# Order of TensorE's steps in an attention pair: the second score group directly behind the first, the third ahead of the mixing

## The chip, the cores and the metric

One core of one Trainium2 chip. The metric is the device time of one execution in microseconds; for the kernel before it is the median of three runs.

## What is computed

Causal attention over 2 batches, 12 heads, 448 tokens and head size 64, then a token-and-channel-mixing block, then a block with a Fourier transform over tokens and channels, a normalisation and a two-layer perceptron, all in fp32:

```python
scores = scale * np.matmul(q, k.transpose(0, 1, 3, 2))
scores = np.where(mask, -1000000000.0, scores)
attn = softmax(scores)                      # rows: exp(s - max) / (sum + 1e-9)
x = np.matmul(attn, v)                      # to (batch, token, channel)
h = np.maximum(x.transpose(0, 2, 1) @ w_tok1, 0.0) @ w_tok2
u = x + h.transpose(0, 2, 1)
x = u + np.maximum(u @ w_ch1, 0.0) @ w_ch2
u = x + real(fft(fft(x, tokens), channels))
out = u + np.maximum(norm(u) @ w2_ch1, 0.0) @ w2_ch2
```

(The softmax, norm and fft lines are abbreviated.)

## The kernel before

Values are split into a high and a low part in a rounded fp32 type, and a product is three passes: high x high, high x low, low x high. The channel weights of the blocks come as 64-bit words and are converted on the chip: `convert_steps` (L77) is one ScalarE instruction (L83), then VectorE's L85 and L86, L90, L94, then a ScalarE copy (L100) and a GpSimd subtraction (L101).

**Attention stage.** The 24 (batch, head) problems are done as 12 pairs. A pair n goes through these steps:

- `prep(n)` (L221): loads q and k by two DMAs on SP's queue and splits them: ScalarE L229 and L231, GpSimd L230, VectorE L235.
- `scores(n, g)` (L243) for the three score groups g = 0, 1, 2. The 448 query rows are four blocks of 112; by causality block i needs only the first 112 (i + 1) keys. Group 0 is blocks 0 and 1, group 1 is block 2, group 2 is block 3. Each group does its matmuls (L261) for both heads, adds the mask by small matmuls (L274), then VectorE reduces for the negative maximum (L278) and ScalarE takes the exponentials with their sums (L287, one instruction and one read of the accumulator per block and head: four in group 0, two in the others).
- `transposes(n, u)` (L292), u = 0 to 4: five groups of four 112x112 transposes of the exponentials on TensorE (L300), each copied out of its bank, for u = 1, 3 by ScalarE (L305), for u = 0, 2, 4 by VectorE (L307), into the one buffer `pt`.
- `pv(n)` (L309): P times V in 16 matmuls (L315), of which the second half reads transposed groups 2 to 4; ScalarE copies the result out (L320).
- `finish(n)` (L322): four transposes back (L336), division by the row sums on VectorE (L332, L333, L338), a split by VectorE L344 and GpSimd L345.

The steps of different pairs are interleaved in the loop at L465. In iteration n the scores are those of pair n, the transposes those of pair n - 1, P times V and `finish` those of pair n - 2. `next_mix()` (L407) takes one step of the token-mixing block off a list that is filled after every third pair: `mix_first` and `mix_second` in iterations 5, 8 and 11 (matmuls L361, evacuated by ScalarE L367 and VectorE L368, and transposes L373 copied by ScalarE L376), and three `mix_out` (L395, added by VectorE L397) in the two iterations after. `weights(after)` (L455) issues one third of the conversion of one weight tile, behind the instructions named, each on its own engine: `mark[2]` is the last score reduction traced (VectorE) and `mark[3]` the last exponential (ScalarE); the number of such steps in an iteration is in `parts` (L461).

**What sets the order.** TensorE's instructions run in the order in which the loop calls them (L464). The order of the other engines is chosen by the framework's planner from priorities, estimated durations and dependencies, and is fixed when the program is built. PSUM has eight banks. Score groups take turns at two pairs of banks (`spair`, L143; in pair 0 group 2 takes two single ones); everything else in this stage takes turns at the other four (`ybank`, L140). Whoever takes a bank waits until what was in it has been read.

The order of TensorE in one iteration before (for 2 <= n < 12): score group 0 of n; P times V of n - 2; score group 1 of n; transposed groups 0 and 1 of n - 1; a mixing step, if any; transposed group 2; score group 2 of n; transposed groups 3 and 4; a mixing step; the transposes of `finish(n - 2)`.

Of the kernel before, what the change touches and what calls it, by code (L numbers as in the profile page):

```python
# [43 lines left out]
def fused_kernel(ctx: ExitStack, tc: tile.TileContext, qk, v, w1, w2, wa, wb, wc, wd, fa, fa0, fb, out):  # L44
# [7 lines left out]
    def small(pool, tag, **kw):  # L52
        t = pool.tile([TS, 16], F32, tag=tag, name=tag, **kw)
        return t[:, : 2 * NI].rearrange("p (i e o) -> p i e o", e=2, o=1)
# [17 lines left out]
    def fetch(src):  # L72
        w = stage_pool[0].tile(list(src.shape), I64, tag="w", name="w", bufs=2)
        nc.sync.dma_start(out=w, in_=src)
        return w
# [64 lines left out]
    def ybank():  # L140
        return psum[:, take("y", 4)]

    def spair():  # L143
        k = 4 + 2 * take("s", 2)
        return psum[:, k : k + 2]
# [41 lines left out]
    with ExitStack() as actx:  # L187
# [33 lines left out]
        def prep(n):  # L221
            c = Pair()
            pairs[n] = c
            b, hp = n // 6, n % 6
            c.kh, c.kl, c.qh, c.ql = [kq.tile([128, S], F32R, tag=t, name=t) for t in ("kh", "kl", "qh", "ql")]
            k32, q32 = stage(n), stage(n)
            nc.sync.dma_start(out=k32, in_=qk[b, hp, :, 1])
            nc.sync.dma_start(out=q32, in_=qk[b, hp, :, 0])
            act.copy(c.kh, k32)  # L229
            (pool if n else vec).tensor_tensor(out=c.kl, in0=k32, in1=f(c.kh), op=ALU.subtract)  # L230
            act.activation(out=c.qh, in_=q32, func=AF.Copy, scale=0.125)  # L231
            with ExitStack() as order:
                if n == 1:
                    order.enter_context(tc.issue_after(mark[2]))
                vec.scalar_tensor_tensor(  # L235
                    out=c.ql, in0=q32, scalar=0.125, in1=f(c.qh), op0=ALU.mult, op1=ALU.subtract
                )
# [5 lines left out]
        def scores(n, g):  # L243
            c = pairs[n]
            if g == 0:
                c.ssum = small(tiny, "ssum")
                c.nmx = small(ap, "nmx")
                c.p = ap.tile([TS, 2, 1120], F32, tag="p", name="p")
            if n or g < 2:
                sp = spair()  # L250
                se = [sp[:TS, e] for e in range(2)]
            else:
                se = [ybank()[:TS] for e in range(2)]
            cols = ((256, 0), (0,), (0,))[g]
            blocks = ((0, 1), (2,), (3,))[g]
            for i, c0 in zip(blocks, cols):
                w = max(256, TS * (i + 1))
                for m, (qt, kt) in enumerate(((c.qh, c.kh), (c.qh, c.kl), (c.ql, c.kh))):
                    for e in range(2):
                        he = slice(D * e, D * e + D)  # L260
                        mm(  # L261
                            se[e][:, c0 : c0 + w], lhsT=qt[he, i * TS : (i + 1) * TS], rhs=kt[he, :w],
                            start=m == 0 and i != 1, stop=False, skip_group_check=True,
                        )
            for hb in range(2):
                for e in range(2):
                    he = slice(D * e, D * e + TS // 2)
                    if g == 0:
                        dst = se[e][:, TS : TS + 288].rearrange("p (i n) -> p i n", i=2)[:, :, :TS]
                        rhs = maskb[he, hb]  # L270
                    else:
                        dst = se[e][:, blocks[0] * TS : (blocks[0] + 1) * TS]
                        rhs = maskb[he, hb, 0]
                    mm(dst, lhsT=identb[he, hb], rhs=rhs, start=False, stop=hb == 1, skip_group_check=True)  # L274
            for i, c0 in zip(blocks, cols):
                w = TS * (i + 1)
                if n or g < 2:
                    mark[2] = vec.tensor_reduce(  # L278
                        out=c.nmx[:, i], in_=sp[:TS, :, c0 : c0 + w], axis=AX.X, op=ALU.max, negate=True
                    ).ins  # L280
                else:
                    for e in range(2):
                        vec.tensor_reduce(out=c.nmx[:, i, e], in_=se[e][:, :w], axis=AX.X, op=ALU.max, negate=True)
            for i, c0 in zip(blocks, cols):
                w = TS * (i + 1)
                for e in range(2):
                    mark[3] = act.activation(  # L287
                        out=c.p[:, e, OFF[i] : OFF[i] + w], in_=se[e][:, c0 : c0 + w], func=AF.Exp,
                        bias=c.nmx[:, i, e], scale=1.0, accum_out=c.ssum[:, i, e],
                    ).ins  # L290

        def transposes(n, u):  # L292
            c = pairs[n]
            if u == 0:
                c.pt = ap.tile([TS, 5, S], F32, tag="pt", name="pt", bufs=1)
            tv = ybank()
            col = 0
            for e, j in (((0, 0),), ((1, 0),), ((0, 1), (0, 3)), ((1, 1), (1, 3)), ((0, 2), (1, 2)))[u]:
                for i in range(j, NI):
                    nc.tensor.transpose(  # L300
                        tv[:TS, col : col + TS], c.p[:, e, OFF[i] + j * TS : OFF[i] + (j + 1) * TS], ident[:TS, :TS]
                    )
                    col += TS
            if u in (1, 3):
                mark[1] = act.copy(c.pt[:, u], tv[:TS, :S]).ins  # L305
            else:
                mark[0] = vec.tensor_copy(c.pt[:, u], tv[:TS, :S]).ins  # L307
# [92 lines left out]
        def split(ct, b):  # L400
            act.copy(act_h[ct][b], resid[ct][b])
            pool.tensor_tensor(out=act_l[ct][b], in0=resid[ct][b], in1=f(act_h[ct][b]), op=ALU.subtract)
# [4 lines left out]
        def next_mix():  # L407
            if mix:
                fn, n, k = mix.pop(0)
                fn(n, k)  # L410
                if fn is mix_out and k == 2:
                    for x in late:
                        split(*x)
                    late.clear()
# [40 lines left out]
        def weights(after):  # L455
            with ExitStack() as order:
                for ins in after:
                    order.enter_context(tc.issue_after(ins))
                next(work, None)
# [4 lines left out]
        with tc.manual_schedule(engines={mybir.EngineType.PE}):  # L464
            for n in range(np_ + 2):  # L465
                live, old = n < np_, 1 <= n <= np_
                if live:
                    scores(n, 0)
                if n + 1 < np_:
                    prep(n + 1)  # L470
                if n in (1, 2):
                    raw.append(fetch(sources[n - 1][0]))
                after = mark[2:4]
                if n >= 2:
                    after.append(pv(n - 2))
                if live and parts[n]:
                    weights(after)
                if live:
                    load_v(n)
                    scores(n, 1)  # L480
                if old:
                    transposes(n - 1, 0)
                    transposes(n - 1, 1)
                next_mix()
                if n == np_:
                    early_up(0)
                if old:
                    transposes(n - 1, 2)
                if live and parts[n] > 1:
                    weights(mark[2:4])  # L490
                if not live:
                    for _ in range(parts[n]):
                        weights(mark[:2])
                if live:
                    scores(n, 2)
                if old:
                    transposes(n - 1, 3)
                    transposes(n - 1, 4)
                if n == np_:
                    early_up(1)  # L500
                next_mix()
                if n == np_ + 1:
                    early_up(2)
                if n >= 2:
                    finish(n - 2)
                if n == np_ + 1:
                    early_up(3)
                if n >= 2 and (n - 2) % 3 == 2:
                    hn = (n - 2) // 3
                    mix += [(mix_first, hn, 0), (mix_second, hn, 1)] + [(mix_out, hn, pr) for pr in range(3)]  # L510
            early_down(0)
            while mix:
                next_mix()
            early_down(1)
# [352 lines left out]
```

## Time and profile before

| | us |
|---|---|
| three runs | 717.93, 718.05, 719.10 |
| median | 718.05 |
| profiled execution | 717.51 |
| its span, first to last instruction | 715.70 |
| TensorE busy in the span | 695.1 (97%) |
| VectorE, ScalarE, GpSimd busy | 526.6, 282.8, 276.7 |

The attention stage with its loop of pairs takes roughly the first 125 us. In the rows, PE is TensorE's matmuls, PEld its weight loads, DVE VectorE, ACT ScalarE, POOL GpSimd, SPq the queue of SyncE; L followed by a number is a line of the kernel. A bracket behind a row of a timeline is the idle time of the engine just before it and what ended it.

### The profile page before, as it was taken

How to read it: one execution, taken by the hardware profiler on the slowest of the kernel's cores; microseconds unless marked ns; L12 is line 12 of the kernel's file. 1: busy time of each engine (PE TensorE's matmuls, PEld its weight loads, DVE VectorE, ACT ScalarE, POOL GpSimd, SP SyncE). 2: the span in 40 equal slices, each digit the busy share in tenths (PEclk: the TensorE clock that was granted, in tenths of full speed). 3: DMA queues.
4: the chain of work that ended last, by engine and by line, in shares of the span. 5: the costliest groups of instructions: out<-in, count | busy, mean ns of one | idle time of the engine just before them, and what ended most of it. 6: DMA issues, size and time to landing. Idle time of an engine off the chain costs nothing.

```text
span 715.7 us, 10290 instructions
## 1 busy us (share of the span) xinstructions
PE 695.1 (97%) x3940; PEld 629.0 (88%) x3940; DVE 526.6 (74%) x808; ACT 282.8 (40%) x600; POOL 276.7 (39%) x197
## 2 busy tenths in 40 slices
PE   6989899999999999999799999999999999999997
PEld 5677787899999999998699999999999999999996
DVE  6899898554898884779879896767855676944722
ACT  7867777323324333133444452233432323432200
POOL 3235553345332422332195335465313556311210
PEclk9999999999999999999999999999999999999999
DMA  8232412128434342200022442433412343322311
GB/s 265 69 116 96 147 35 82 59 69 224 170 119 147 118 146 90 89 1 0 1 89 88 125 140 90 138 127 118 144 62 81 126 140 126 118 88 95 105 51 52
DMA packets 20608, 74.15 MB, mean 104 GB/s; under 512 B 2364, under 2 KB 6974, under 8 KB 20192
## 3 DMA queue, kind: packets, MB, share of 16 engines
q1 hardware_dynamic: 19952, 69.48, 29.5%
q0 software_dynamic: 608, 4.03, 2.1%
q8 instruction: 31, 0.51, 0.3%
q14 instruction: 17, 0.14, 0.1%
HBM read 70.75 MB, written 2.75 MB: 103 GB/s over the span
## 4 chain that ended last, share of the span: by engine, by line
PE 81%; DVE 10%; ACT 5%; issue 2%; POOL 1%; DMA 0%; ACTq 0%; POOLq 0%; DVEq 0%
PE psum L164 12%; PE psum L163 12%; PE psum L162 12%; PE psum L181 11%; PE psum L180 11%; PE psum L179 11%; PE psum L261 3%; ACT p L287 2%; PE psum L315 2%; PE psum L300 2%; PE psum L395 2%; PE psum L361 1%; DVE nmx L278 1%; DVE resid L655 1%; POOL wl L101 1%
## 5 line engine op out<-in xcount | busy, mean ns | idle before, releaser
L101 POOL TENSOR_TENSOR wl<-m,wh 128x512 fp32r<-128x512 f32 (+1 forms) x90 | 150.1, 1668 | 257.2 <-ACT wh L100 240.6
L180 PE MATMUL psum<-gh,wl 128*128 128x448 f32 x432 | 156.6, 363 | 0.0
L163 PE MATMUL psum<-acth,wl 128*128 128x448 f32 x432 | 156.6, 363 | 0.0
L164 PE MATMUL psum<-actl,wh 128*128 128x448 f32 x432 | 156.4, 362 | 0.0
L181 PE MATMUL psum<-gl,wh 128*128 128x448 f32 x432 | 156.4, 362 | 0.0
L162 PE MATMUL psum<-acth,wh 128*128 128x448 f32 x432 | 156.2, 361 | 0.0
L179 PE MATMUL psum<-gh,wh 128*128 128x448 f32 x432 | 156.2, 361 | 0.0
L83 ACT ACTIVATE m<-w 128x512 f32<-128x512 f32 (+2 forms) x92 | 71.3, 775 | 164.5 <-POOL wl L101 123.1
L85 DVE TENSOR_SCALAR m<-m 128x512 f32<-128x512 f32 (+2 forms) x92 | 48.8, 532 | 77.7 <-ACT m L83 77.6
L90 DVE SCALAR_TENSOR_TENSOR m<-w,m 128x512 uint32<-128x512 uint32 (+2 forms) x92 | 101.6, 1105 | 2.4
L94 DVE SCALAR_TENSOR_TENSOR m<-w,m 128x512 uint32<-128x512 uint32 (+2 forms) x92 | 98.8, 1075 | 1.6
L100 ACT CAST wh<-m 128x512 fp32r<-128x512 f32 (+1 forms) x90 | 63.4, 704 | 90.5 <-DVE m L94 50.2
L162 PEld LDWEIGHTS psum<-acth,wh 128*128 128x128 f32 x432 | 80.9, 187 | 5.8
L163 PEld LDWEIGHTS psum<-acth,wl 128*128 128x128 f32 x432 | 81.1, 188 | 5.6
L180 PEld LDWEIGHTS psum<-gh,wl 128*128 128x128 f32 x432 | 81.1, 188 | 5.6
L179 PEld LDWEIGHTS psum<-gh,wh 128*128 128x128 f32 x432 | 80.9, 187 | 5.8
L164 PEld LDWEIGHTS psum<-actl,wh 128*128 128x128 f32 x432 | 81.0, 188 | 4.8
L181 PEld LDWEIGHTS psum<-gl,wh 128*128 128x128 f32 x432 | 81.0, 187 | 4.8
L166 DVE SCALAR_TENSOR_TENSOR gl<-psum,gh 128x448 fp32r<-128x448 f32 x72 | 43.9, 616 | 25.1 <-ACT gh L165 25.1
L165 ACT ACTIVATE gh<-psum 128x448 fp32r<-128x448 f32 x72 | 37.6, 539 | 61.7 <-PE psum L164 61.7
L86 DVE TENSOR_SCALAR m<-m 128x512 uint32<-128x512 uint32 (+2 forms) x92 | 54.7, 596 | 2.3
L287 ACT ACTIVATE p<-psum,nmx 112x112 f32<-112x112 f32 (+3 forms) x96 | 46.9, 508 | 24.0 <-DVE nmx L278 23.1
(151 smaller groups left out, 855.2 us busy)
## 6 DMA issues: line engine op xcount, KB each, us to landing
w<-in_wc SPq DMA_DIRECT2D x24, 768.0 KB, 4.3
w<-in_wd SPq DMA_DIRECT2D x36, 512.0 KB, 3.4
w<-in_wa SPq DMA_DIRECT2D x12, 768.0 KB, 4.3
w<-in_wb SPq DMA_DIRECT2D x18, 512.0 KB, 3.3
resid<-in_qk SPq DMA_DIRECT2D x24, 224.0 KB, 2.7
v<-in_v SPq DMA_DIRECT2D x12, 224.0 KB, 3.1
out<-t SPq DMA_DIRECT2D x12, 224.0 KB, 1.9
w<-in_w SPq DMA_DIRECT2D x2, 896.0 KB, 9.8
```

Of the source, the lines that this page charges most:

```text
L83: act.activation(out=m, in_=hi.bitcast(F32), func=AF.Abs)
L90: vec.scalar_tensor_tensor(out=mu, in0=lo, scalar=29, in1=mu, op0=ALU.logical_shift_right, op1=ALU.bitwise_or)
L94: vec.scalar_tensor_tensor(out=mu, in0=hi, scalar=0xC0000000, in1=mu, op0=ALU.bitwise_and, op1=ALU.bitwise_or)
L100: act.copy(wh, m)
L101: pool.tensor_tensor(out=wl, in0=m, in1=f(wh), op=ALU.subtract)
L162: mm(pb[:, :S], lhsT=lh, rhs=act_h[ct][b], start=ct == 0, stop=False)
L163: mm(pb[:, :S], lhsT=ll, rhs=act_h[ct][b], start=False, stop=False)
L164: tail[0] = mm(pb[:, :S], lhsT=lh, rhs=act_l[ct][b], start=False, stop=ct == NCT - 1).ins
L179: mm(pb[:, :S], lhsT=lh, rhs=gh, start=j + k == 0, stop=False)
L180: mm(pb[:, :S], lhsT=ll, rhs=gh, start=False, stop=False)
L181: tail[0] = mm(pb[:, :S], lhsT=lh, rhs=gl, start=False, stop=j == last and k == nk - 1).ins
L287: mark[3] = act.activation(out=c.p[:, e, OFF[i] : OFF[i] + w], in_=se[e][:, c0 : c0 + w], func=AF.Exp, bias=c.nmx[:, i, e], scale=1.0, acc ...
```

## The change

In the loop, `scores(n, 1)` is called directly behind `scores(n, 0)`, ahead of `prep(n + 1)` and P times V; `scores(n, 2)` is called behind transposed groups 0 and 1, ahead of the first mixing step and of transposed group 2. Since `mark` keeps the last reduction and exponential traced, the first conversion step of an iteration now follows score group 1 instead of 0, and the second follows group 2 instead of 1.

```diff
                 if live:
                     scores(n, 0)
+                    scores(n, 1)
                 if n + 1 < np_:
                     prep(n + 1)
...
                 after = mark[2:4]
                 if n >= 2:
                     after.append(pv(n - 2))
                 if live and parts[n]:
                     weights(after)
                 if live:
                     load_v(n)
-                    scores(n, 1)
                 if old:
                     transposes(n - 1, 0)
                     transposes(n - 1, 1)
+                if live:
+                    scores(n, 2)
                 next_mix()
                 if n == np_:
                     early_up(0)
...
                 if not live:
                     for _ in range(parts[n]):
                         weights(mark[:2])
-                if live:
-                    scores(n, 2)
                 if old:
                     transposes(n - 1, 3)
                     transposes(n - 1, 4)
```

## Rows read from the trace of the kernel before

**Rows 1.** The page: its first line and the line of busy shares.

```profile
span 715.7 us, 10290 instructions
PE 695.1 (97%) x3940; PEld 629.0 (88%) x3940; DVE 526.6 (74%) x808; ACT 282.8 (40%) x600; POOL 276.7 (39%) x197
```

**Rows 2.** Waits of TensorE: who for whom, us in total, times, longest.

```profile
PE psum L300 <- DVE actl L368: 2.0, 2, 1.6
PE psum L315 <- DVE pt L307: 1.7, 1, 1.7
PE psum L261 <- ACT p L287: 1.7, 3, 1.2
PE psum L336 <- ACT pt L305: 0.8, 1, 0.8
PE psum L336 <- DVE resid L397: 0.6, 2, 0.3
```

**Rows 3.** Stretches: us; busy (count) of PE, PEld, DVE, ACT, POOL; clock; DMA.

```profile
41.00:58.00 17.00, 15.04 (x112) 12.51 (x111) 15.34 (x19) 11.43 (x35) 7.84 (x5) 0.90 0.34 114
...
145.00:300.00 155.00, 155.00 (x787) 145.47 (x786) 116.00 (x171) 51.15 (x83) 52.69 (x36) 1.00 0.42 135
```

**Rows 4.** Timeline of TensorE, iteration 6: start, us, line, operation, out and in.

```profile
59.62 2.11 PE L315 MATMUL psum<-pt,v 112*64 112x448 f32 x16
61.66 0.41 PE L261 MATMUL psum<-kh,qh 64*112 64x336 f32 x2
...
62.41 0.98 PE L300 MATMUL psum<-ident,p 112*112 112x112 f32 x8
63.16 0.65 PE L395 MATMUL psum<-w2h,acth 128*128 128x448 f32 x2
...
64.46 0.55 PE L300 MATMUL psum<-ident,p 112*112 112x112 f32 x4
64.94 0.46 PE L261 MATMUL psum<-kh,qh 64*112 64x448 f32 x2
...
65.84 0.98 PE L300 MATMUL psum<-ident,p 112*112 112x112 f32 x8
```

**Rows 5.** Timeline of TensorE: waits in pairs 1, 3 and 5.

```profile
13.98 0.88 PE L261 MATMUL psum<-kh,qh 64*112 64x448 f32 x2 [1.16 <-ACT p L287]
...
29.11 0.89 PE L261 MATMUL psum<-kh,qh 64*112 64x448 f32 x2 [0.26 <-ACT p L287]
...
30.44 1.12 PE L300 MATMUL psum<-ident,p 112*112 112x112 f32 x8
...
46.01 0.79 PE L315 MATMUL psum<-pt,v 112*64 112x224 f32 x8 [1.70 <-DVE pt L307]
```

**Rows 6.** Timelines of VectorE and ScalarE, iteration 6: score group 0.

```profile
60.55 0.91 DVE L278 TENSOR_REDUCE nmx<-psum 112x2 f32<-112x224 f32 x2
...
63.01 0.21 ACT L287 ACTIVATION_READ_ACCUMULATOR p<-psum,nmx 112x1 f32 x1
```

**Rows 7.** Timelines of VectorE and GpSimd, iterations 4 and 5.

```profile
40.62 3.81 DVE L86 TENSOR_SCALAR m<-m 128x896 uint32<-128x896 uint32 x1
44.35 1.08 DVE L278 TENSOR_REDUCE nmx<-psum 112x2 f32<-112x896 f32 x1
45.35 0.61 DVE L307 COPY pt<-psum 112x448 f32<-112x448 f32 x1
...
47.35 0.91 DVE L278 TENSOR_REDUCE nmx<-psum 112x2 f32<-112x224 f32 x2
40.23 2.62 POOL L101 TENSOR_TENSOR w1l<-m,w1h 112x1024 fp32r<-112x1024 f32 x1 [4.05 <-ACT w1h L100]
42.80 1.15 POOL L230 TENSOR_TENSOR kl<-resid,kh 128x448 fp32r<-128x448 f32 x1
```

**Rows 8.** Timelines of TensorE and ScalarE, iteration 2.

```profile
17.29 2.11 PE L315 MATMUL psum<-pt,v 112*64 112x448 f32 x16
17.61 0.74 ACT L287 ACTIVATE p<-psum,nmx 112x448 f32<-112x448 f32 x1
```

## What the change should do to the time

> **What bounds the kernel now.** I read the page's busy shares first: TensorE is busy 695.1 of 715.7 us [rows 1], so only what makes it wait can move the time, for the change adds and removes no instruction. Next, who makes TensorE wait [rows 2]. These five lie in the attention stage, which the change reorders, and sum to 2.0 + 1.7 + 1.7 + 0.8 + 0.6 = 6.8 us. Then the table of stretches [rows 3]: in iteration 5 (41 to 58 us) TensorE is busy 15.04 of 17 us at a mean granted clock of 0.90, so 17 - 15.04 = 2.0 us idle and 0.10 x 17 = 1.7 us lost to the lower clock, 3.7 us together. VectorE is busy 15.34 of those 17 us: it is nearly as full as TensorE, and its order decides who waits. From 145 to 300 us TensorE has no idle time at all, so what the attention stage wins or loses is passed on whole.
>
> Last, TensorE's own order in an undisturbed iteration [rows 4]: P times V takes 61.66 - 59.62 = 2.04 us, the second score group 0.75, transposed groups 0 and 1 together 0.75, group 2 alone 0.48, the third score group 0.90. After a wait a score group costs more than the wait: the third group of pair 3 takes 30.44 - 29.11 = 1.33 us instead of 0.90 [rows 5], its weight loads having begun only then too. So every wait ahead of a score group carries 0.43 us extra. With three such waits all recoverable loss is about 6.8 + 3 x 0.43 + 1.7 = 9.8 us, 1.4% of the time. That is the floor for any gain.
>
> **The change, part by part.** TensorE's work and count, the DMAs of the q, k and v loads on SP's queue and the subtractions on GpSimd stay as they are, in the same order among themselves; a score group issues no DMA, so nothing is moved past those queues. TensorE's order is written by hand; VectorE and ScalarE are ordered by the planner. Two steps of weight conversion are tied to the most recent reduction and exponential when they are called, so the first step now stands behind the second group's and the second behind the third's, each one score group later than before.
>
> *Added wait 1, third group on first.* Two bank pairs serve three groups, so the third needs the first's four exponentials done. The way between them on TensorE is now 0.75 + 2.04 + 0.75 = 3.54 us, in every iteration; before it had group 2 and the mixing work on top. On the other side, pair 6 needs 2.45 us from the start of the first group's reduction (60.55) to the start of the last accumulator read (63.01) [rows 6]. So the reduction may start 3.54 - 2.45 = 1.1 us after the matmuls end; in pair 6 it started 60.55 - 59.62 = 0.9 us after. That just holds. Behind a waiting third group stand the mixing matmuls and three transposed groups.
>
> *Added wait 2, second group on the previous third.* The same ring. In pair 2 the previous third group's exponentials end at 17.61 + 0.74 = 18.35 us [rows 8], while TensorE is through with the first group at 17.29, where P times V starts, and with pair 1's 0.48 of delay (below) at 17.8: up to 0.6 us. P times V queues behind it. Elsewhere the previous third group comes earlier by group 2 and the mixing, and covers this.
>
> *Iterations 1 to 4.* Pair 1's wait of 1.16 us [rows 5] hid group 2, which now comes after it: +0.48. Pair 2: a wait of 0 to 0.6 us by the above plus 0.43: I take +0.6 (0 to 1.0), nearest to that row. Pair 3: waits of 0.26 and 0.79 us (the latter is the 0.8 of rows 2) and 0.43 for the reload stood there; VectorE sets the time of the exponentials, so what pairs 1 and 2 lost is partly taken up: -0.5 (-1.5 to +0.5). Pair 4: the remaining wait of 1.7 - 1.16 - 0.26 = 0.28 and its 0.43 mostly go, since the third group's reduction leaves the late part of pair 3: -0.4 (-0.7 to +0.5). Together +0.18.
>
> *Iteration 5.* One VectorE instruction of the conversion ran from 40.62 for 3.81 us; GpSimd ran at 40.23 for 2.62 and at 42.80 for 1.15, so VectorE ended 0.48 us after GpSimd did [rows 7]. Behind it stood pair 4's third reduction, then the copy of group 4 (45.35 to 45.96), for which P times V waited until 46.01 [rows 5]. Now that reduction stands ahead of the conversion, so the copy comes 45.35 - 44.43 = 0.9 to 1.0 us earlier, and the second score group is already done: 1.0 + 0.75 = 1.75 us won. The first group's reduction, at 47.35 before, moves with it to about 46; its exponentials end near 48.4, while TensorE, resuming at 45.0, finishes P times V (0.7) and groups 0 and 1 (0.75) at 46.5: a new wait of 1.9 + 0.43 = 2.3 us. Net +0.6. The lower clock, 1.7 us, follows idle time of the engine in the rows; with as much idle in the new order I give it an even chance: -0.9. Sum -0.3; ends -3.7 (all that rows 3 show lost) and +2.3 (the copy no earlier, both waits).
>
> [...] The rows show VectorE waiting through two GpSimd instructions in a row. [...]
>
> *Iterations 6 and 9.* The first mixing result must leave its bank three groups later, without the third score group (0.90) between: +0.1 each (0 to 0.5).
>
> *Iterations 7 and 10.* The last transposes wait for the mixing result's addition on VectorE, 0.6 us over both [rows 2], which stands behind a conversion step; so does the addition in the new order. The third group no longer stands between, so 0.90 us of cover goes, half of which the conversion's own later place may give back: +0.45 each (0 to 0.9).
>
> *Iterations 8 and 11.* Group 4 waited 1.6 and 0.4 us [rows 2] for the mixing input's split; ScalarE did the second group's exponentials ahead of it. Those come earlier now, but 0.90 us of cover goes: 8: -0.6 (-1.9 to +0.6), 11: +0.1 (-0.4 to +0.9).
>
> Sum: 0.18 - 0.3 + 0.2 + 0.9 - 0.6 + 0.1 = +0.5 us. The profiled execution took 717.51 us (span 715.70); that becomes 718.0. The median of the runs is 0.54 us higher; I name 718.4, a little under 718.05 + 0.5.
>
> **The rivals.** *Faster: VectorE's late part is relieved.* The third reduction and the split of q leave the crowded end of an iteration; if then the first group's exponentials are always in time, iteration 5 gives up its 3.7 us and iteration 8 its 1.6, against +0.5 and +0.6 in pairs 1 and 2: -4.2 us, 713.8. For it: VectorE's 15.34 of 17 us and the reduction queued behind the held conversion [rows 3, 7]. Against: VectorE's total is the same, and the conversion still meets GpSimd.
>
> *Slower: the third group waits for the first group's exponentials in the bulk of iterations.* It decides from the point where the reduction starts over 1.1 us late; pair 6 is at 0.9 now, and pair 3, whose third group waited even behind group 2, is past it. At 0.2 us of wait and 0.43 of reload in seven iterations (3 and 6 to 11) that is 7 x 0.63 = +4.4 us, 722.4. For it: thin cover. Against: less stands ahead of the first reduction on VectorE.
>
> *The planner leaves the other engines' order nearly as it is.* Then only the small shifts of pairs 1 and 7 remain, under 1.4 us, which ends within no change.
>
> **How the numbers follow.** About 0.2%, 1.4 us, is what a measurement of this kernel can tell from no change. My forecast (offsetting waits, the planner's case and the port rule's -0.6 with it) gets 0.36; faster 0.34, as iteration 5 holds the largest single loss; slower 0.30. The range reaches to both rivals: 713.8 to 722.6, leaving about 0.1 out on each side. The likeliest case's own range is 716.6 to 719.5.
>
> **What would show it.** Right: TensorE's waits total about the same, with "third group on the first's exponentials" in place of "P times V on the copy of group 4" at iteration 5, and the wait of the last transposes in 7 and 10 grown from 0.6 to about 1.5 us together. Wrong to the fast side: no wait over 1 us in 41 to 58 us and a clock of 1.00 there. Wrong to the slow side: waits of score groups on exponentials in six or more iterations, summing to over 4 us, or a second stretch at the lower clock.

## The result, and the profile after

| | before | after |
|---|---|---|
| median of the runs, us | 718.49 | 725.23 (724.6 to 726.5) |
| ratio | 1 | 1.0096 [1.0078, 1.0113] |
| profiled execution, us | 717.51 | 725.16 |
| its span, us | 715.7 | 723.4 |

(The runs of before were repeated beside those of after, hence 718.49.) The change makes the kernel slower by about 1%, 2.6 us above the range. The page of after, first line and busy shares:

```profile
span 723.4 us, 10303 instructions
...
PE 699.6 (97%) x3940; PEld 632.6 (87%) x3940; DVE 523.2 (72%) x808; ACT 282.1 (39%) x600; POOL 276.8 (38%) x197
```

Against [rows 1] TensorE is busy 4.5 us longer with the same 3940 matmuls: part of the loss is not waiting but the same work at a lower clock (mean granted clock over the span 0.993 in before, 0.989 in after). The waits of TensorE in after, as in [rows 2]:

```profile
PE psum L261 <- ACT p L287: 5.7, 9, 2.4
...
PE psum L300 <- DVE actl L368: 2.9, 3, 1.8
PE psum L395 <- DVE resid L397: 0.8, 2, 0.4
...
PE psum L336 <- ACT pt L305: 0.4, 1, 0.4
```

P times V's wait for the copy of group 4 (1.7 us) and that of the last transposes for the addition (0.6) are gone; score groups wait 4.0 us more for exponentials, transposed groups 0.9 more for the mixing split, and the mixing step L395 0.8. To find the place I took the length of each iteration, from the start of `finish`'s transposes (L336) in the iteration before to that in it, beside the term that the prediction had for it:

| us | before | after | difference | predicted |
|---|---|---|---|---|
| pairs 1 and 2 (start of L336 in iteration 2) | 23.09 | 24.39 | +1.30 | +1.08 |
| 3 | 9.27 | 9.64 | +0.37 | -0.5 |
| 4 | 8.28 | 7.97 | -0.31 | -0.4 |
| 5 | 17.26 | 17.04 | -0.22 | -0.3 |
| 6 | 10.00 | 10.39 | +0.39 | +0.1 |
| 7 | 9.08 | 8.78 | -0.30 | +0.45 |
| **8** | **15.19** | **19.47** | **+4.28** | **-0.6** |
| 9 | 9.90 | 10.38 | +0.48 | +0.1 |
| 10 | 9.05 | 8.75 | -0.30 | +0.45 |
| 11 | 13.45 | 13.57 | +0.12 | +0.1 |
| start of L336 in iteration 13 | 146.34 | 152.14 | +5.80 | +0.5 |

Of the profiled difference of 7.65 us, 5.8 arise here, three quarters of them in one iteration; 0.9 more come up to the matmul that takes the mean for the normalisation (L652: 342.70 before, 349.42 after), of which 0.6 is a wait of L181 for VectorE's L166. The last 1.0 goes with a stretch at half clock around the end of the wait for L668 (4.04 us in before, 4.07 in after): from 354.6 to 358.0 us in before, 3.4 us, and from 358.9 to 365.8 in after, 6.8 us. The mean granted clock of the runs of before beside the experiments went from 0.987 to 0.995, so I do not put it down to the change.

The stretch of iteration 8 in before, then iterations 5 and 8 in after (columns as in [rows 3]):

```profile
76.98:92.17 15.19, 13.30 (x112) 10.97 (x113) 12.36 (x21) 11.39 (x32) 8.25 (x6) 1.00 0.31 97
```

```profile
42.00:59.04 17.04, 14.05 (x114) 11.39 (x113) 13.99 (x24) 11.66 (x34) 7.99 (x5) 1.00 0.43 147
...
78.21:97.68 19.47, 16.30 (x115) 13.85 (x114) 14.12 (x24) 11.52 (x34) 8.87 (x7) 0.82 0.31 101
```

Length less busy time is idle time: in iteration 8 it grows from 15.19 - 13.30 = 1.89 us to 19.47 - 16.30 = 3.17, by 1.28; the other 3.00 us are busy time at a mean clock of 0.82 (0.18 x 19.47 = 3.5 us). The granted clock is at half, 0.50, from 85.87 to 92.70 us. What TensorE did just before it fell stands in the timeline of after (TensorE, then VectorE, then GpSimd, then ScalarE):

```profile
79.66 0.39 PE L261 MATMUL psum<-kh,qh 64*112 64x336 f32 x2
...
82.43 0.98 PE L300 MATMUL psum<-ident,p 112*112 112x112 f32 x8
85.78 1.14 PE L261 MATMUL psum<-kh,qh 64*112 64x448 f32 x2 [2.37 <-ACT p L287]
...
94.35 0.60 PE L300 MATMUL psum<-ident,p 112*112 112x112 f32 x4 [0.80 <-DVE actl L368]
...
80.63 0.61 DVE L235 SCALAR_TENSOR_TENSOR ql<-resid,qh 128x448 fp32r<-128x448 f32 x1
81.16 1.36 DVE L344 CAST xh<-x 112x512 fp32r<-112x512 f32 x1
...
82.51 0.38 DVE L278 TENSOR_REDUCE nmx<-psum 112x2 f32<-112x224 f32 x1
82.81 1.09 DVE L348 CAST xh<-xh 112x4 fp32r<-112x4 f32 x1
83.81 1.38 DVE L278 TENSOR_REDUCE nmx<-psum 112x2 f32<-112x448 f32 x2
...
77.07 2.09 POOL L101 TENSOR_TENSOR wl<-m,wh 128x768 fp32r<-128x768 f32 x1 [1.23 <-ACT wh L100]
79.11 1.47 POOL L230 TENSOR_TENSOR kl<-resid,kh 128x448 fp32r<-128x448 f32 x1
80.55 1.69 POOL L402 TENSOR_TENSOR actl<-resid,acth 128x448 fp32r<-128x448 f32 x1
82.60 1.28 POOL L345 TENSOR_TENSOR xl<-x,xh 112x512 fp32r<-112x512 f32 x1 [0.36 <-DVE xh L344]
...
84.52 0.35 ACT L287 ACTIVATE p<-psum,nmx 112x112 f32<-112x112 f32 x1 [4.03 <-DVE nmx L278]
```

Read it backwards. The third score group waits 2.37 us, until 85.78, for the first group's exponentials; ScalarE, idle 4.03 us, could not begin these until 84.52 for want of the reduction; VectorE did that in two halves, at 82.51 and at 83.81 (that row joins the second half, 0.61 us, with the second group's reduction), though the first group's matmuls ended at 79.66, where the second group's start. Ahead of the halves and between them stand two instructions much longer than their like: the cast of xh, 1.36 us, and the one-column copy L348, 1.09 us for 112x4 elements. Each ends shortly after a GpSimd instruction does (82.52 after L402's 82.24, 83.90 after L345's 83.88). The same place in before, TensorE, VectorE and GpSimd:

```profile
78.64 2.11 PE L315 MATMUL psum<-pt,v 112*64 112x448 f32 x16
...
80.25 0.41 DVE L344 CAST xh<-x 112x512 fp32r<-112x512 f32 x1
...
80.66 0.38 DVE L278 TENSOR_REDUCE nmx<-psum 112x2 f32<-112x224 f32 x1
80.96 1.10 DVE L348 CAST xh<-xh 112x4 fp32r<-112x4 f32 x1
81.97 0.61 DVE L278 TENSOR_REDUCE nmx<-psum 112x2 f32<-112x448 f32 x1
...
74.15 1.83 POOL L101 TENSOR_TENSOR wl<-m,wh 128x768 fp32r<-128x768 f32 x1 [1.21 <-ACT wh L100]
77.60 1.15 POOL L402 TENSOR_TENSOR actl<-resid,acth 128x448 fp32r<-128x448 f32 x1 [1.62 <-ACT acth L401]
78.70 1.14 POOL L230 TENSOR_TENSOR kl<-resid,kh 128x448 fp32r<-128x448 f32 x1
80.74 1.29 POOL L345 TENSOR_TENSOR xl<-x,xh 112x512 fp32r<-112x512 f32 x1 [0.90 <-DVE x L347]
```

Here GpSimd was idle from 79.84 to 80.74 and the cast of xh, falling into that gap, took 0.41 us. In after there is no gap. The weight subtraction (`wl`) is ahead of `actl` in both kernels, but it had ended at 75.98 in before, 1.0 us ahead of iteration 8, and ends at 79.16 in after, 0.95 us into it; and `kl` now stands ahead of `actl`, not behind it. So `actl` runs until 82.24, and the cast was held 1.36 - 0.41 = 0.95 us. (The copy L348 was held in both kernels; a copy of the same size, L347, takes 0.16 us, so 0.93 of its 1.09 are held time.) **GpSimd's order and timing changed**, though the change moves only score groups and, through `mark`, conversion steps.

The rows of before show one thing more. Its own pair 8 was late already: the first group's matmuls end at 78.64, its reduction starts at 80.66 and ends at 81.97 + 0.61 = 82.58, 3.94 us behind them. TensorE did not wait, because the third group came only at 85.74 there; in after the lateness is 83.81 + 0.61 - 79.66 = 4.76 us. Most of the lateness is old; the cover is what went.

### The profile page after: what moved, and what is told of

Read it like the earlier page. It is cut to its first block, busy times and chain, and to the rows that moved or that the text cites. A ratio compares the mean times of both kernels' runs of the same rounds, so it can differ in the third digit from the quotient of the medians.

```text
span 723.4 us, 10303 instructions
## 1 busy us (share of the span) xinstructions
PE 699.6 (97%) x3940; PEld 632.6 (87%) x3940; DVE 523.2 (72%) x808; ACT 282.1 (39%) x600; POOL 276.8 (38%) x197
## 3 DMA queue, kind: packets, MB, share of 16 engines
q0 software_dynamic: 608, 4.03, 2.1%
## 4 chain that ended last, share of the span: by engine, by line
PE 71%; DVE 17%; ACT 6%; issue 2%; DMA 2%; POOL 1%; ACTq 0%; DVEq 0%; POOLq 0%; SPq 0%
PE psum L164 10%; PE psum L163 10%; PE psum L162 10%; PE psum L181 10%; PE psum L180 9%; PE psum L179 9%; DVE m L90 3%; ACT p L287 3%; PE psum L261 2%; PE psum L361 2%; PE psum L315 2%; DVE m L94 2%; DVE m L85 2%; PE psum L395 1%; PE psum L300 1%
## 5 line engine op out<-in xcount | busy, mean ns | idle before, releaser
L181 PE MATMUL psum<-gl,wh 128*128 128x448 f32 x432 | 156.8, 363 | 0.6 <-DVE gl L166 0.6
L85 DVE TENSOR_SCALAR m<-m 128x512 f32<-128x512 f32 (+2 forms) x92 | 49.7, 541 | 81.4 <-ACT m L83 81.4
L181 PEld LDWEIGHTS psum<-gl,wh 128*128 128x128 f32 x432 | 81.1, 188 | 5.9 <-DVE gl L166 1.0
L166 DVE SCALAR_TENSOR_TENSOR gl<-psum,gh 128x448 fp32r<-128x448 f32 x72 | 43.8, 615 | 24.0 <-ACT gh L165 24.0
L165 ACT ACTIVATE gh<-psum 128x448 fp32r<-128x448 f32 x72 | 37.5, 540 | 56.5 <-PE psum L164 56.4
L772 POOL TENSOR_TENSOR resid<-t,resid 128x448 f32<-128x448 f32 x24 | 33.7, 1403 | 49.5 <-DVE t L771 49.5
```

The costliest lines, as they stand in the source:

```text
L85: vec.tensor_scalar(out=m, in0=m, scalar1=F64_MIN, scalar2=F64_MAX, op0=ALU.max, op1=ALU.min)
L181: tail[0] = mm(pb[:, :S], lhsT=lh, rhs=gl, start=False, stop=j == last and k == nk - 1).ins
```

## The experiments

The account to be tested: (1) pair 8's third group now waits on a reduction that VectorE reaches late because GpSimd holds it, and the clock falls after that wait; (2) the planner changed GpSimd's and ScalarE's order, since a third group done earlier frees the q and k buffers earlier, and splits of a later pair go ahead of mixing work. (That the freed buffers are why the planner did so is read from the program and not tested; what the new order costs is.) The rivals: the loss is in the second group's move, in the weight conversion's later places, or spread over the iterations. All kernels compute everything. Ratios are to runs of before beside each, with medians of 719.54 us (719.31 for edge, from5, tied_copies and part1_copies); compare kernels by ratios, not by us.

**The two moves apart.** part1 moves the second group alone, part2 the third alone:

```diff
 part1: before, with
                     scores(n, 0)
+                    scores(n, 1)
...
-                    scores(n, 1)
 part2: before, with
                     transposes(n - 1, 1)
+                if live:
+                    scores(n, 2)
...
-                if live:
-                    scores(n, 2)
```

> The kernel before with the second score group directly behind the first and nothing else moved. Theory A: the third group keeps its old cover (mixing and transposed group 2) and waits for no exponentials over 0.5 us except in pair 1; no clock drop at 86 us; within 2 us of the kernel before. Theory B: about half of the 6.9 us, 3 to 4 us slower than before.

> The kernel before with the third score group behind transposed groups 0 and 1 and nothing else moved (the second group stays behind P times V). The third group has the same 3.54 us of cover on the first group as in the change. Theory A: pair 8's third group waits over 1.5 us with a clock drop after it, and the kernel is 4 us or more slower than before. Theory B: 3 to 4 us slower, without one dominant wait.

part1: 718.88 us, ratio 0.9997 [0.9986, 1.0008], level. Its iteration 5 takes 14.46 us instead of 17.26, but pairs 1 and 2 lose 1.2 us and iteration 4 1.0, and score groups wait for exponentials far oftener (4.9 us in 14 waits, the longest 1.0, that of pair 8's second group on pair 7's third). part2: 722.94 us, ratio 1.0054 [1.0035, 1.0072], between level and the full change. Its timeline of TensorE:

```profile
56.05 0.60 PE L300 MATMUL psum<-ident,p 112*112 112x112 f32 x4 [1.82 <-DVE actl L368]
...
86.59 0.89 PE L261 MATMUL psum<-kh,qh 64*112 64x448 f32 x2 [1.06 <-ACT p L287]
...
93.27 0.60 PE L300 MATMUL psum<-ident,p 112*112 112x112 f32 x4 [1.82 <-DVE actl L368]
```

More than half of the loss comes with the third group's move alone, and none with the second group's alone; the rest takes both. The new wait of group 4 in iteration 5 (1.82 us) comes with the third group too (the one in iteration 8 was 1.60 in before). So does GpSimd's order: part2 has `kl` (79.26) ahead of `actl` (81.37) as after has, part1 `actl` (77.12) ahead of `kl` (78.60) as in before. In pair 8 the third group waits 1.06 us here, 2.37 in the full change, and the clock stays full behind that wait (four matmuls of L361, at 88.72, take 0.87 us); part2's half-clock stretches in the attention stage stand elsewhere (at 15.5, 56.5 and 94 us, 3.4 us each; the same four matmuls, at 94.66, take 1.49 us). So theory A missed here, in the size of the wait and in the clock; the loss, 0.54% or 3.9 us, is what theory B had named. The cast of xh was free here (0.42 us) in spite of the new GpSimd order, and pair 8 waited all the same.

**Pair 8's third group at its old place.**

```diff
-                if live:
+                if live and n != 8:
                     scores(n, 2)
                 next_mix()
...
+                if n == 8:
+                    scores(n, 2)
```

> The changed kernel, but in iteration 8 alone the third score group stands at its old place, behind the first mixing step and transposed group 2. Theory A (the loss is one wait, that of pair 8's third group on its first group's exponentials, 2.37 us, and the lower clock that follows it, 6.8 us at half speed): the wait goes below 0.5 us, the clock stays at full from 80 to 95 us, iteration 8 takes about 15.2 us instead of 19.5, and the time falls by 4 us or more, to 721 or below. Theory B (the loss is spread: cover gone in every iteration): the wait moves to the next step of iteration 8, the time falls by under 1.5 us.

721.29 us, ratio to before 1.0036 [1.0018, 1.0055], by the ratios 0.6% or 4.3 us faster than after; iteration 8 takes 15.76 us, and the clock is full there (L361's groups of four matmuls take 0.86 to 0.97 us), as theory A expected. But 0.5, 1.35 and 0.5 us of other waits appeared in it and 0.9 in iteration 9; and iteration 5, ahead of the edited one, took 18.61 us instead of 17.04, with a stretch at half clock from 57.0 us (the four matmuls at 57.42 take 1.49 us) behind the wait of 1.84 us that after has too (1.82), without one. So the wait of pair 8 costs about what was supposed, 3.7 us net with its clock (19.47 to 15.76), but taking it out by TensorE's order brings others.

**Pair 8's casts off VectorE.** In copies, `finish(5)`, called at the end of the loop's iteration 7, so that its VectorE work meets pair 8's first score group, does its cast of xh and the two one-column copies on ScalarE; in edge the one-column copies alone go there:

```diff
-            vec.tensor_copy(h.h[:, :, sl], h.x[:, :, sl])
+            (act.copy if n == 5 else vec.tensor_copy)(h.h[:, :, sl], h.x[:, :, sl])
...
+                edge_copy = act.copy if n == 5 else vec.tensor_copy
-                vec.tensor_copy(h.x[:, :, 0:1], h.x[:, :, 384:385])
-                copied = vec.tensor_copy(h.h[:, :, 0:1], f(h.h)[:, :, 384:385])
+                edge_copy(h.x[:, :, 0:1], h.x[:, :, 384:385])
+                copied = edge_copy(h.h[:, :, 0:1], f(h.h)[:, :, 384:385])
```

> The changed kernel, but three copies of pair 5's finish (the split's high part and the two one-column copies) are done by ScalarE instead of VectorE. Theory A, in its second part (the wait of 2.37 us is there because the first reduction of pair 8 stands on VectorE behind copies that are held while GpSimd runs, 1.36 and 1.09 us where such copies take 0.41 and 0.16 elsewhere): the reduction of pair 8 ends about 2 us earlier, the wait falls to under 0.7 us, the clock stays at full, the time falls by 3.5 to 5 us. If it is rather that VectorE has too much work there whatever it is: the wait falls by about the 0.7 us of work moved, to 1.6 us, and the clock drop stays; the time falls by 1 us or less.

> The changed kernel with only the two one-column copies of pair 5's finish on ScalarE; the wide copy of the split's high part stays on VectorE. In the changed kernel the second of the one-column copies stood between the two halves of pair 8's first reduction and took 1.09 us, and the wide copy 1.36 us, both held by GpSimd. If held time simply adds on VectorE ahead of the reduction: the wait of 2.37 us falls by 1.1 to 1.3 us, to about 1.1, the lower clock after it may go, and the time falls by 1.5 to 4 us. If the wide copy alone matters (it is first in the queue): the wait stays above 2 us.

copies: 720.53 us, ratio 1.0027 [1.0015, 1.0039]. Its stretch of iteration 8 and its timeline of VectorE and ScalarE there:

```profile
79.80:94.60 14.80, 13.67 (x115) 11.17 (x113) 11.55 (x21) 12.16 (x37) 11.68 (x7) 1.00 0.41 136
```

```profile
82.75 0.91 DVE L278 TENSOR_REDUCE nmx<-psum 112x2 f32<-112x224 f32 x2
...
83.75 0.35 ACT L287 ACTIVATE p<-psum,nmx 112x112 f32<-112x112 f32 x1 [0.57 <-DVE nmx L278]
```

The two halves of the reduction stand together, the wait is gone, the clock is 1.00 and iteration 8 is 4.67 us shorter than in after; by the ratios 0.7% or 5 us are won back, as theory A expected. GpSimd's order is still that of after, so what hurt was the held VectorE instructions and not GpSimd's lateness. edge: 722.36 us, ratio 1.0040 [1.0026, 1.0055], iteration 8 16.19 us. Its timeline of TensorE and VectorE:

```profile
84.82 0.88 PE L261 MATMUL psum<-kh,qh 64*112 64x448 f32 x2 [1.30 <-ACT p L287]
...
81.27 1.36 DVE L344 CAST xh<-x 112x512 fp32r<-112x512 f32 x1
```

With L348 off VectorE the wait falls by 2.37 - 1.30 = 1.07 us, about that instruction's whole 1.09; with the cast of xh (1.36) off too the rest goes. The lengths of the two add, held time and work together. (In edge the clock falls to half behind the shorter wait too, for 3.4 us instead of 6.8: the mean of iteration 8 is 0.89 where it is 0.82 in after.)

**The planner's new order undone.** In tied, the splits of three pairs wait for a mixing instruction: those of pairs 7 and 10 for the mixing ReLU, those of pair 9 for the last mixing split. (The lines of this kernel are 9 to 11 higher.)

```diff
+                key = {7: 'first', 10: 'first', 9: 'split'}.get(n)
+                if key:
+                    order.enter_context(tc.issue_after(behind[key]))
...
+            relu = act.activation(out=th, in_=hp[:, :384], func=AF.Relu).ins
+            if t == 0:
+                behind['first'] = relu
...
+            behind['split'] = act.copy(act_h[ct][b], resid[ct][b]).ins
```

> The changed kernel, but the q and k splits of pairs 7 and 10 are placed behind the first mixing ReLU of iterations 5 and 8 on each engine's order, and those of pair 9 behind the last mixing split of iteration 7. Theory C (the third group, done earlier, frees the q and k buffers earlier; the splits of pair n + 2 then jump ahead of the mixing work on ScalarE and GpSimd, and that is what makes transposed group 4 wait 1.82 us at iteration 5 and keeps GpSimd busy when pair 8's copies come): group 4's wait at iteration 5 falls by about 0.9 us (two splits of 0.47 us) to under 1.0; pair 8's wait of 2.37 us falls to under 1.2 us; the time falls by 2 us or more. Rival (the splits only fill time; the cover of 0.9 us that the third group gave is what is missing): both waits change by under 0.5 us.

721.35 us, ratio 1.0031 [1.0019, 1.0043]. Half of what theory C expected came: the time fell by 0.65% and group 4's wait too, but not pair 8's. (In the profiles 2.3 of the 4.0 us come from the attention stage; the rest goes with less time at half clock: iteration 8 is at 0.82 in both, and the mean of the span is 0.993 in tied, 0.989 in after.) In after ScalarE did the splits of pair 7 (L229, L231), and the third group's exponentials behind them, ahead of the mixing ReLU of iteration 5:

```profile
51.95 0.61 ACT L229 CAST kh<-resid 128x448 fp32r<-128x448 f32 x1
52.42 0.62 ACT L231 ACTIVATE qh<-resid 128x448 fp32r<-128x448 f32 x1
...
54.11 0.54 ACT L367 ACTIVATE acth<-psum 128x384 fp32r<-128x384 f32 x1
```

In tied (timeline of TensorE, VectorE, GpSimd, ScalarE):

```profile
84.42 1.14 PE L270 MATMUL psum<-kh,qh 64*112 64x448 f32 x2 [2.34 <-ACT p L296]
...
79.28 1.53 DVE L244 SCALAR_TENSOR_TENSOR ql<-resid,qh 128x448 fp32r<-128x448 f32 x1
80.73 0.42 DVE L353 CAST xh<-x 112x512 fp32r<-112x512 f32 x1
...
81.44 1.09 DVE L357 CAST xh<-xh 112x4 fp32r<-112x4 f32 x1
82.45 1.38 DVE L287 TENSOR_REDUCE nmx<-psum 112x2 f32<-112x448 f32 x2
...
79.20 1.13 POOL L239 TENSOR_TENSOR kl<-resid,kh 128x448 fp32r<-128x448 f32 x1
...
53.18 0.55 ACT L376 ACTIVATE acth<-psum 128x384 fp32r<-128x384 f32 x1
```

The ReLU comes 0.93 us earlier, and group 4's wait of 1.82 us falls to 0.48; iteration 5 takes 15.70 us. So the early splits on ScalarE are the cause of most of that wait. But pair 8 still waits 2.34 us: with `kl` put behind `actl` it met the subtraction for `ql` instead, 1.53 us in place of 0.61, and the cast of xh went free at 0.42. The held time changed its victim and kept its size (0.92 + 0.93 = 1.85 us, against 0.95 + 0.93 = 1.88 in after). So the order of `kl` and `actl` is not what decides pair 8's wait.

**The conversion at its old neighbours.** marks ties the first two conversion steps to score groups 0 and 1, as they were before the change:

```diff
                     scores(n, 0)
+                    tied = mark[2:4]
                     scores(n, 1)
+                    tied2 = mark[2:4]
...
-                after = mark[2:4]
+                after = list(tied) if live else mark[2:4]
...
-                    weights(mark[2:4])
+                    weights(tied2)
```

> The changed kernel, but the two conversion steps of an iteration are tied to the score groups they were tied to before (first and second instead of second and third). If the conversion's later place carries part of the loss, VectorE's conversion instructions come about 1 us earlier in each iteration, the wait at pair 8 falls by 1 us or more and the time falls by 2 us or more. Theory A with C (held copies and the q and k splits): the conversion's place matters little, within 1.5 us of the changed kernel unless it happens to move GpSimd's run off the copies.

725.31 us, ratio 1.0092 [1.0072, 1.0112]: as after. But pair 8's wait is gone. GpSimd and VectorE in marks:

```profile
76.50 1.83 POOL L101 TENSOR_TENSOR wl<-m,wh 128x768 fp32r<-128x768 f32 x1 [2.05 <-ACT wh L100]
...
81.63 0.11 DVE L348 CAST xh<-xh 112x4 fp32r<-112x4 f32 x1
```

`wl` starts 2.9 us ahead of iteration 8 again (at 79.40), as in before (2.8 us) and not as in after (1.1 us), and pair 8's two casts run free (0.41 and 0.11 us). So the conversion's later place, a part of the change, is what made `wl` late; for the casts a second thing may count, for TensorE also reaches pair 8 later here, the last transposes ahead of it having waited 1.14 us. Against that group 4 waits 6.6 us in three waits (2.50 at 55.93, 2.47 at 91.46). The conversion's later place carries no net cost: moved back, the waits change theirs.

**The early iterations.** early58 is before with the second group early in pairs 5 and 8 only; from5 is tied_copies (below) with the old order up to pair 4.

```diff
 early58: before, with
                     scores(n, 0)
+                    if n in (5, 8):
+                        scores(n, 1)
...
-                    scores(n, 1)
+                    if n not in (5, 8):
+                        scores(n, 1)
 from5: tied_copies, with
+                    if n > 4:
+                        scores(n, 1)
...
+                if live and n > 4:
+                    scores(n, 2)
...
+                if n < 5:
+                    scores(n, 2)
```

> The kernel before with the second score group directly behind the first in iterations 5 and 8 alone. With that move in every iteration, iteration 5 took 14.46 us instead of 17.26 and iteration 8 14.89 instead of 15.19, while iterations 2 and 4 lost 1.2 and 1.0 us. If iterations add up: 2.5 to 3.1 us faster than the kernel before, that is a ratio near 0.996. If a win in one iteration is given back in the next: within 1 us of it.

> As the kernel with both the copies and the ties, but with the new order of score groups only from iteration 5 on. Pairs 1 and 2 keep their old order, in which transposed group 2 fills pair 1's wait: if the 1.3 us lost there is due to the order, iteration 2 ends at 23.1 us as before, and the time is 1 to 2 us under that of the kernel with both everywhere. If a late VectorE passes it on anyway (iteration 5 takes longer when it starts earlier): within 0.7 us of it.

Both missed: early58 721.46 us, 1.0031 [1.0019, 1.0043], from5 721.88, 1.0035 [1.0021, 1.0048]. The timeline of early58, TensorE and VectorE:

```profile
47.26 1.23 PE L261 MATMUL psum<-kh,qh 64*112 64x336 f32 x2 [3.38 <-ACT p L287]
...
41.66 3.79 DVE L86 TENSOR_SCALAR m<-m 128x896 uint32<-128x896 uint32 x1
45.37 1.08 DVE L278 TENSOR_REDUCE nmx<-psum 112x2 f32<-112x896 f32 x1
```

In before the held conversion of [rows 7] delayed a copy that P times V needed, 1.7 us. With the second group early in pair 5 and pair 4's third group still late, the same held instruction stands ahead of pair 4's third reduction, and the second group waits 3.38 us for its exponentials. from5 has the same wait, and in both the clock is at half behind it: P times V's 16 matmuls take 3.63 and 3.61 us there, 2.11 in [rows 4]. part1, with the second group early in all pairs, has no such wait, so the early order in pairs 1 to 4, which costs 1.2 to 1.3 us at the start, is what keeps it away: the pairs could not be chosen one by one. (Iteration 2 ended at 24.6 us in both, not at 23.1 as expected, for another reason than the order: pair 1's wait of 1.16 us, in before the same and in from5 1.15, was followed here by 3.4 us at half clock: the eight transposes behind the third group take 1.74 us, 0.98 in before.)

**The repairs together, and without the change.** tied_copies is after with both repairs, part1_copies is part1 with copies, copies_before is the kernel before with copies.

> The changed kernel with both: the three copies on ScalarE and the q and k splits behind the mixing. If the two causes add (iteration 8 from 19.47 to 14.8 us by the copies, iteration 5 from 17.04 to 15.7 by the tie): 5 to 7 us faster than the changed kernel, 718.5 to 720 us, level with the kernel before or up to 1 us slower, the rest being pairs 1 and 2 (1.3 us). If they share one cause: no faster than either alone, 720.5 to 721.4 us.

> The kernel before with the second score group directly behind the first everywhere and the three copies on ScalarE. Second group alone was level with the kernel before (ratio 0.9997), the copies alone 0.9979. If they add: 717.5 us. If pair 8's second group, which waited 0.97 us on exponentials, also gains from the copies: a ratio of 0.996 to 0.997.

> The kernel before with the three copies of pair 5's finish on ScalarE. There the first of them was not held (0.41 us) and the last was (1.10 us), and no score group of pair 8 waited on exponentials. Theory A: what the copies cost was paid only in the new order, so here the gain is at most the waits of iteration 8 (0.29 and 1.60 us): 0 to 1.9 us faster. If the copies are a general cost of VectorE's queue: the same 4 us gain as in the changed kernel.

| | us | ratio to before | iteration 5 | iteration 8 |
|---|---|---|---|---|
| tied_copies | 718.35 | 0.9984 [0.9973, 0.9995] | 15.70 | 14.80 |
| part1_copies | 718.01 | 0.9976 [0.9963, 0.9990] | 14.46 | 16.08 |
| copies_before | 717.58 | 0.9979 [0.9968, 0.9991] | 17.28 | 13.98 |

The two repairs nearly add: by the ratios copies gives back 0.7% of the time, tied 0.65%, both 1.1%, a little more than the 5 to 7 us expected. Together they undo the change's loss and little more. (In tied_copies pair 8's third group still waits 0.93 us, for `ql` is held as in tied.) The same move of small casts gains 0.2% in the kernel before too, where L348 was held (1.10 us) between the halves of pair 8's reduction as well; the second group's early place makes no difference to that within the intervals. part1_copies and copies_before beat both kernels, narrowly, as their expectations had it.

## Why the prediction was wrong

**The step that failed** is added wait 1 as it was applied. It was weighed in pair 6 alone ("in pair 6 it started 60.55 - 59.62 = 0.9 us after. That just holds"), and the term for iteration 8, -0.6, holds group 4 only: a wait of the third group there stood at nothing, without a reason. By the rows of before shown above, pair 8's reduction starts 80.66 - 78.64 = 2.0 us after the matmuls, past the prediction's own limit of 1.1 us; with the limit worked out below its 3.94 us of lateness alone would be a wait of 1.5 us in the new order. Measured were 2.37 us and half clock behind them.

**A second step failed**, and made it worse: "the subtractions on GpSimd stay as they are, in the same order among themselves". They are the same subtractions, but the planner put `kl` ahead of `actl`, and the conversion's later place, which the prediction had named, made `wl` late. In pair 8 that holds the cast of xh and takes the lateness from 3.94 to 4.76 us; copies shows that without the held instructions the wait is gone, tied and part2 that it does not hang on the order of `kl` and `actl`. In iteration 5 tied shows that the new order makes most of group 4's wait. Pairs 5 and 8 were costed on the old neighbours.

**Added wait 1 was the right mechanism**, and its threshold was near: "the reduction may start 1.1 us after the matmuls end". The runs give it more exactly. From the end of the first group's matmuls to the third group, TensorE has 3.75 us of other work (after: 85.78 - 2.37 - 79.66), and from the end of the reduction's second half to the third group are 1.36 us (after: 85.78 - 84.42, with 0.61 for a half of 448 elements as in before). So the reduction may end 2.4 us after the matmuls, that is start 1.5 us after them when it is not cut in two (0.91 us). The prediction had 0.2 us too little cover (3.54) and 0.2 too long a chain: the third group starts at 85.78, ahead of the last accumulator read, which starts at 85.95. The test, with the wait as lateness less 2.4 ("matmuls end" is where TensorE's next step starts):

| pair 8 in | matmuls end | reduction ends | late | wait by this | measured |
|---|---|---|---|---|---|
| after | 79.66 | 83.81 + 0.61 | 4.76 | 2.36 | 2.37 |
| tied | 78.32 | 82.45 + 0.61 | 4.74 | 2.34 | 2.34 |
| edge | 79.78 | 82.55 + 0.91 | 3.68 | 1.28 | 1.30 |
| copies | 81.25 | 82.75 + 0.91 | 2.41 | 0.01 | none |
| part2 | 81.77 | 84.63 + 0.61 | 3.47 | 1.07 | 1.06 |
| tied_copies | 78.77 | 81.19 + 0.91 | 3.33 | 0.93 | 0.93 |

(The 2.4 is fitted on after; the other five lines test it.) Without its 0.95 + 0.93 = 1.88 us of held time pair 8 would still be 0.5 us late. But pair 6 in after has its reduction end 1.2 us after the matmuls (60.82 + 0.91 - 60.50) and pair 7 2.2 us (72.20 + 0.91 - 70.87), both in time, so the rival "in the bulk of iterations" was right in kind and wrong in number: not 7 x 0.63 us, but once 2.37 us, and some 3 us of clock on top, which no rival had priced. The prediction's own signs for the slow side came: score groups wait for exponentials in six pairs (1 to 5 and 8), 5.7 us together.

**Iteration 8**, forecast at -0.6, measured +4.28: the part that was weighed came (group 4's wait fell from 1.60 to 0.80 us), the third group was not weighed, and no price was put on a lower clock after a new wait; the prediction weighed the clock at iteration 5 only.

**Iteration 5** came out as forecast (-0.22 for -0.3), but by other parts, so that is luck. P times V's wait is gone (1.70 us) and the lower clock with it (mean 1.00, 0.90 in before), so that busy time falls to 14.05 us from 15.30. In their place stand the third group's wait (0.69 us at 49.05, where 1.9 was expected) and group 4's 1.82 us, which the prediction had for pairs 8 and 11 only; with two short ones of the second group they are the 17.04 - 14.05 = 2.99 us of idle time. No run shows "the port rule's -0.6", which the chances count with the forecast; what the runs showed in its place is VectorE held through both GpSimd instructions in before (3.81 us) and, in after, held through the first alone, until 0.49 us past its end.

**Iterations 1 to 4**: +1.30 for pairs 1 and 2 against +1.08, and -0.31 for 4 against -0.4, hold; for 3 the +0.37 lies inside its ends. **7 and 10** were forecast at +0.45 each and gained 0.30 each: the wait of the last transposes for the addition did not grow to 1.5 us, it vanished, and waits for the same additions (L397) of 0.40 and 0.36 us stand instead at the mixing step L395 in 6 and 9, whose +0.39 and +0.48 stand within their ends. "What the attention stage wins or loses is passed on whole" held nearly: 5.8 us became 6.7 at L652.

## What to carry to other kernels

Where a planner orders the engines beside the one whose order is written by hand, a step that frees a buffer earlier changes their order too: list what waits for that buffer, and where the planner may put it, before costing the step. A cover that is taken away must be checked against every pair's rows, not one pair's: here pair 8's, in before, would have shown the wait. On an engine that is nearly full, look for tiny instructions that stand between the parts of a reduction and run long; moving one such cast and two copies to an engine with idle time gained 0.2% here under the old order, where the new order by itself lost 1%. And a wait is priced with the clock that may follow it, which in pair 8 was the larger part (3.00 of 4.28 us).

## What the runs showed of the hardware

**VectorE held by GpSimd, in both orders.** In before VectorE's L86 lasted through two GpSimd instructions in a row, 3.81 us [rows 7], where it took 1.02 us in after. In after another step of the same conversion went in between the two; its timeline of VectorE and GpSimd:

```profile
42.52 1.93 DVE L85 TENSOR_SCALAR m<-m 128x896 f32<-128x896 f32 x1
...
41.57 2.39 POOL L101 TENSOR_TENSOR w1l<-m,w1h 112x1024 fp32r<-112x1024 f32 x1 [3.71 <-ACT w1h L100]
43.91 1.53 POOL L230 TENSOR_TENSOR kl<-resid,kh 128x448 fp32r<-128x448 f32 x1
```

L85 took 1.93 us, 0.61 in before; it ended at 44.45, 0.49 us after the first GpSimd instruction (43.96), and the second took 1.53 us where it took 1.15 in before: now GpSimd was the one held. So VectorE was held through both in before, and in after through the first alone. In tied `ql` took 1.53 us on VectorE beside GpSimd's `kl`, 1.13 us; in after it took 0.61 beside `actl`, which then took 1.69 us where it took 1.15 in before: there GpSimd was the one held.

**The same wait, with and without a lower clock.** Group 4's wait of 1.82 to 1.85 us in iteration 5 was followed by half clock in late8 and copies (iteration 5: 18.6 us) and in part2 (18.3), not in after and edge (17.0 us). Stretches at half clock that ended within the span of the two profiles lasted 3.4 us in before (from 47.4 and 354.6 us) and 6.8 us in after (from 85.9 and 358.9). So a single profile does not settle what a wait costs; after and copies differ by 1.6 us in an iteration that lies ahead of their difference.
